# An attention and mixer kernel on one core: token-weight loads behind the first keys, the last product in two halves, a new list of places

## The chip, the cores and the metric

The kernel runs on one core of a Trainium2 chip. The metric is the device time of one execution in microseconds (us); less is better. The times before are from three runs, the profile is one more execution of the same program.

## The reference

Four batches, 12 heads, 448 positions, 64 numbers a head. Causal attention, then a mixer over the positions ("tokens") and one over the 768 channels, both with a residual:

```python
scores = np.where(mask, -1e9, scale * np.matmul(q, k.transpose(0, 1, 3, 2)))
scores = scores - np.max(scores, axis=-1, keepdims=True)
attn = np.exp(scores)
attn = attn / (np.sum(attn, axis=-1, keepdims=True) + 1e-09)
out = np.matmul(attn, v)                       # (B, H, S, D)
x = out.transpose(0, 2, 1, 3).reshape(B, S, H * D)
xt = x.transpose(0, 2, 1)
h = np.maximum(xt @ w_tok1, 0.0) @ w_tok2      # 448 -> 256 -> 448
u = x + h.transpose(0, 2, 1)
h2 = np.maximum(u @ w_ch1, 0.0) @ w_ch2        # 768 -> 1536 -> 768
return u + h2
```

## The kernel before

The heads are worked in 24 pairs, six to a batch. A pair's steps are: load keys, queries and values; turn keys and queries so that the head's 64 numbers lie on the partitions (by VectorE's transpose at L985, or by TensorE at L907 and L913); the scores as small 64x64-tile matmuls (L1018), in two pieces of jobs per pair; for each block of rows "low" (L1040, VectorE: mask and running extreme), the exponential (L1052, ScalarE), a guard and a reciprocal (L1071, L1074) and the scaling; the turn of the probabilities (L1112 on TensorE for the early pairs, through DMA for later ones); the product with the values (L1242, 128x64 tiles, and L1251 for the tips). Of each value load the first rows are copied into a second tile, "vend" (L633 by a helper). Two or more pairs make a slice of x that is turned (L1288) and goes through the token mixer (L1347, relu L1355, L1360, L1380, sum at L1388). The channel mixer works in stages with the up product (L1430 and L1762), and for the last two batches in groups: `group.up` L1833 and `group.down` L1853, whose results are summed into the residual `u` by `add` (L1497). Products are made in three matmuls of 448 columns for a high and a low half of each operand; `narrow` (loads at L685, then L688 on ScalarE, L694 and L698 on VectorE) turns 64-bit weights into such floats.

Channel weights come in loads of 768 KB (`wraw`), keys and queries in four DMAs of 56 KB a tensor (`blocks`, L937; 56 KB as the page counts each), values in three (L946 twice with 96 KB, L950 once), dense rows at L889 and L892. SP issues most DMAs; ScalarE's queue issues some at the start and at the end. The DMAs of these two queues share eight completion semaphores in turn, so that the ninth DMA waits at its queue until the first has landed.

The order of the work is not written out. Every step is a `Job` of a `Plan`; its number in the table `PLACES` is its priority, and a second table, `CHOICE`, gives the engine where several could do it. `Plan.emit` walks a modelled clock, gives each engine the ready job with the lowest number, and so fixes each engine's order of instructions; `keep_warm` (L862) puts filler matmuls into early gaps of TensorE.

At the end of the program the last down products of batches 2 and 3 are handled by `finish` instead of `add`: the sum with the residual in two parts of 224 columns (`plus`, L1875, VectorE), per part the turn by two matmuls on TensorE (L1881), the copy out of PSUM (L631 or L633 by a helper), and a DMA to the output (L1889). The other blocks go by `store`: a transpose on VectorE (L1903) and four DMAs (L1907).

Line numbers here and in the rows are those of the kernel before; in the changed kernel the same lines are one to twelve further down (L685 is L686, L937 is L940, L946 is L949, L1018 is L1021, L1242 is L1245, L1881 is L1893).

Of the kernel before, what the change touches and what calls it, by code (L numbers as in the profile page):

```python
# [21 lines left out]
    "load_pair.blocks": {-2: (1, 2), 10: (124, 153), 12: (201, 252), 14: (234, 266), 16: (288, 343), 18: (405, 422),  # L22
        20: (522, 539), 22: (580, 592), 24: (686, 699), 26: (747, 780), 28: (827, 839), 30: (912, 930), 32: (985,
        1004), 34: (1074, 1080), 36: (1130, 1141), 38: (1204, 1219), 40: (1271, 1331), 42: (1360, 1376), 44: (1404,
        1438)},
    "load_pair.load": {0.5: (8,), 2.5: (9,), 4.5: (174,), 6.5: (219,), 8.5: (306,), 10.5: (332,), 12.5: (392,),
        14.5: (450,), 16.5: (489,), 18.5: (552,), 20.5: (614,), 22.5: (666,), 24.5: (766,), 26.5: (855,), 28.5:
        (899,), 30.5: (971,), 32.5: (1060,), 34.5: (1105,), 36.5: (1192,), 38.5: (1260,), 40.5: (1306,), 42.5:
        (1420,), 44.5: (1489,), 46.5: (1538,)},
    "load_pair.upper": {-0.2: (39,), 1.8: (43,), 3.8: (213,), 5.8: (258,), 7.8: (362,), 9.8: (371,), 11.8: (441,),  # L30
        13.8: (499,), 15.8: (515,), 17.8: (584,), 19.8: (653,), 21.8: (703,), 23.8: (790,), 25.8: (894,), 27.8:
        (928,), 29.8: (1009,), 31.8: (1082,), 33.8: (1131,), 35.8: (1220,), 37.8: (1299,), 39.8: (1329,), 41.8:
        (1449,), 43.8: (1514,), 45.8: (1566,)},
    "narrow.load": {3.5: (0, 3, 19, 52, 60, 102, 106, 150), 12: (282,), 13: (367,), 14: (446,), 15: (508,), 16:
        (606,), 17: (679,), 18: (743,), 19: (819,), 20: (910,), 21: (967,), 22: (1033,), 23: (1100,), 24: (1168,),
        25: (1250,), 26: (1326,), 27: (1400,), 28: (1458,), 29: (1521,), 30: (1564,), 31: (1605,), 32: (1636,), 33:
        (1666,), 34: (1687,), 35: (1723,)},
    "narrow.size": {3.5: (5, 16, 55, 97, 108, 145, 158, 184), 12: (342,), 13: (411,), 14: (490,), 15: (561,), 16:
        (645,), 17: (707,), 18: (775,), 19: (850,), 20: (937,), 21: (1002,), 22: (1071,), 23: (1126,), 24: (1203,),
        25: (1285,), 26: (1364,), 27: (1439,), 28: (1499,), 29: (1550,), 30: (1594,), 31: (1622,), 32: (1653,), 33:  # L40
        (1678,), 34: (1710,), 35: (1743,)},
    "narrow.shift": {3.5: (7, 17, 66, 101, 127, 151, 167, 189), 12: (348,), 13: (427,), 14: (497,), 15: (567,), 16:
        (649,), 17: (712,), 18: (785,), 19: (865,), 20: (946,), 21: (1014,), 22: (1076,), 23: (1133,), 24: (1213,),
        25: (1291,), 26: (1370,), 27: (1446,), 28: (1509,), 29: (1557,), 30: (1599,), 31: (1625,), 32: (1658,), 33:
        (1681,), 34: (1713,), 35: (1751,)},
    "narrow.join": {3.5: (10, 22, 78, 107, 138, 157, 173, 196), 12: (359,), 13: (439,), 14: (501,), 15: (587,), 16:
        (659,), 17: (725,), 18: (788,), 19: (870,), 20: (950,), 21: (1018,), 22: (1077,), 23: (1159,), 24: (1222,),
        25: (1296,), 26: (1372,), 27: (1453,), 28: (1516,), 29: (1558,), 30: (1601,), 31: (1629,), 32: (1664,), 33:
        (1682,), 34: (1716,), 35: (1754,)},
    "token_weights.<lambda>": {3.5: (11, 26, 82, 113, 143, 163, 197, 209)},  # L50
# [482 lines left out]
def kernel(  # L533
# [12 lines left out]
    B, H, S, D = q.shape  # L546
# [1419 lines left out]
```

## Time and profile before

| what | value |
|---|---|
| median of three runs | 543.31 us (542.58 to 543.38) |
| the profiled execution | 543.6 us, of which the span is 541.7 us |
| TensorE clock granted, mean of the profile | 0.999 |
| TensorE busy | 532.4 us (98% of the span), 4377 matmuls |
| VectorE, ScalarE, GpSimd busy | 424.4, 316.2, 164.6 us |
| moved by DMA | 77.72 MB, mean 143 GB/s |

The span runs from the first to the last instruction of the profiled execution, and 1.9 us lie around it. Times in the views are counted from the span's start. PE is TensorE's matmuls, PEld its weight loads, DVE is VectorE, ACT ScalarE, POOL GpSimd, and SPq or ACTq an engine's queue of DMA issues. A row of a timeline gives the start, the duration of the group, and how many instructions it holds; several matmuls run into each other, so that the time one costs is the distance to the next start, not its own duration.

### The profile page before, as it was taken

What the parts mean: (1) busy time and instruction counts of PE and PEld (TensorE: products, weight loads), DVE (VectorE), ACT (ScalarE), POOL (GpSimd) and SP (SyncE); (2) the same over time, 40 slices, a digit from 0 to 9 for tenths busy, and PEclk for the clock granted to TensorE, in tenths of its full rate; (3) what the DMA queues carried; (4) which work ended last, traced back from release to release, by engine and by line L of the source; (5) the groups of instructions that cost most, each with busy time, mean ns of one, the idle gap of its engine ahead of it and who ended that gap; (6) DMA issues with size and microseconds to landing.
All of it is one profiled execution on the core that took longest, in us unless ns stands there. A gap on an engine that the chain in (4) does not pass through costs nothing.

```text
span 541.7 us, 12006 instructions
## 1 busy us (share of the span) xinstructions
PE 532.4 (98%) x4377; PEld 460.3 (85%) x4381; DVE 424.4 (78%) x1032; ACT 316.2 (58%) x765; POOL 164.6 (30%) x221
## 2 busy tenths in 40 slices
PE   7999999999999999999999999999999999999996
PEld 3777887888888888788888999999999999999995
DVE  4997988998998898969878579776787858485664
ACT  4998997999887788978794243343222313141300
POOL 3475744524414413322322353241000310101100
PEclk9999999999999999999999999999999999999999
DMA  8866777999899899889985426648213021212139
GB/s 189 195 119 135 160 221 145 192 198 200 154 233 221 179 186 194 202 186 194 195 242 160 145 88 180 143 120 170 88 30 102 17 87 30 71 50 83 31 55 148
DMA packets 221546, 77.72 MB, mean 143 GB/s; under 512 B 195760, under 2 KB 210992, under 8 KB 221488
## 3 DMA queue, kind: packets, MB, share of 16 engines
q1 hardware_dynamic: 207984, 74.90, 61.3%
q10 hardware_dynamic: 13504, 2.07, 2.4%
q8 instruction: 34, 0.56, 0.4%
q14 instruction: 24, 0.20, 0.1%
HBM read 49.15 MB, written 14.94 MB: 118 GB/s over the span
## 4 chain that ended last, share of the span: by engine, by line
PE 94%; DMA 2%; SPq 2%; ACT 1%; issue 0%; DVE 0%; DVEq 0%
PE ps L1430 33%; PE ps L1853 16%; PE ps L1762 12%; PE ps L1018 7%; PE ps L1242 6%; PE ps L1347 6%; PE ps L1380 6%; PE ps L1833 3%; PE ps L1112 2%; PE ps L1251 2%; PE ps L1288 1%; SPq L937 1%; DMA gl<-in_q_dram 1%; DMA kq<-in_q_dram 1%; DMA wl<-in_moe_w_tok_dram 1%; ACT prob L1052 1%
## 5 line engine op out<-in xcount | busy, mean ns | idle before, releaser
L1497 DVE TENSOR_TENSOR u<-ps,u 128x448 f32<-128x448 f32 x118 | 72.6, 621 | 42.3 <-PE ps L1853 31.0
L1052 ACT ACTIVATE prob<-prob,stat 128x192 f32<-128x192 f32 (+6 forms) x168 | 83.9, 502 | 13.4 <-DVE stat L1040 12.4
L1040 DVE CUSTOM_DVE_ANT_0 prob<-ps,mask 128x320 f32<-128x320 f32 (+6 forms) x168 | 63.6, 414 | 7.3 <-PE ps L1018 6.8
L633 POOL TENSOR_SCALAR prob<-prob,stat 128x64 f32<-128x64 f32 (+6 forms) x86 | 44.3, 527 | 67.2 <-DVE stat L1074 55.4
L631 ACT ACTIVATE wh<-wf 128x768 fp32r<-128x768 f32 x24 | 19.9, 843 | 63.3 <-PE ps L1853 36.3
L1430 PE MATMUL ps<-uh,wh 128*128 128x448 f32 x144 | 54.1, 376 | 0.0
L1430 PE MATMUL ps<-gh,wh 128*128 128x448 f32 x144 | 53.4, 371 | 0.0
L1430 PE MATMUL ps<-gl,wh 128*128 128x448 f32 x144 | 52.7, 366 | 0.0
L1430 PE MATMUL ps<-uh,wl 128*128 128x448 f32 x144 | 52.6, 365 | 0.0
L1430 PE MATMUL ps<-ul,wh 128*128 128x448 f32 x144 | 52.6, 365 | 0.0
L1430 PE MATMUL ps<-gh,wl 128*128 128x448 f32 x144 | 52.4, 364 | 0.0
L1018 PE MATMUL ps<-kq,kq 64*64 64x128 f32 (+5 forms) x768 | 45.9, 358 | 1.1 <-DVE kq L633 0.8
L642 POOL TENSOR_TENSOR wl<-wf,wh 128x768 fp32r<-128x768 f32 x20 | 37.7, 1888 | 26.1 <-ACT wh L631 18.7
L1018 PEld LDWEIGHTS ps<-kq,kq 64*64 64x64 f32 x768 | 26.6, 133 | 18.7 <-issue 10.4
L642 POOL TENSOR_TENSOR pt<-wf,u 128x768 fp32r<-128x768 f32 (+1 forms) x5 | 8.4, 1690 | 104.9 <-ACT u L631 76.9
L1242 PE MATMUL ps<-pt,vraw 128*64 128x128 f32 (+2 forms) x544 | 37.8, 285 | 0.0
L637 ACT COPY pt<-pt 128x512 uint16<-128x512 uint16 (+3 forms) x44 | 36.0, 881 | 0.7 <-DMA pt<-prob 0.6
L1242 PEld LDWEIGHTS ps<-pt,vraw 128*64 128x64 f32 x544 | 28.3, 137 | 9.5 <-issue 2.5
L642 POOL TENSOR_TENSOR ul<-u,uh 128x448 fp32r<-128x448 f32 x19 | 24.4, 1296 | 30.5 <-DVE uh L633 23.0
L1052 ACT ACTIVATION_READ_ACCUMULATOR prob<-prob,stat 128x1 f32 x168 | 32.2, 192 | 0.0
L637 ACT COPY prob<-prob 128x1024 uint16<-128x1024 uint16 (+1 forms) x33 | 30.2, 936 | 1.3 <-POOL prob L633 1.3
L1853 PE MATMUL ps<-u,wh 128*128 128x448 f32 x108 | 30.7, 366 | 0.0
(221 smaller groups left out, 1419.2 us busy)
## 6 DMA issues: line engine op xcount, KB each, us to landing
wraw<-in_moe_w_ch_dram SPq DMA_DIRECT2D x24, 768.0 KB, 5.4
wf<-scratch SPq DMA_DIRECT2D x30, 384.0 KB, 3.3
scratch<-wf SPq DMA_DIRECT2D x24, 384.0 KB, 3.9
vraw<-in_v_dram SPq DMA_DIRECT2D x44, 96.0 KB, 3.6
kq<-in_k_dram SPq DMA_DIRECT2D x60, 56.0 KB, 3.4
kq<-in_q_dram SPq DMA_DIRECT2D x56, 56.0 KB, 2.4
out_dram<-h1h SPq DMA_DIRECT2D x24, 56.0 KB, 1.8
out_dram<-h1l SPq DMA_DIRECT2D x24, 56.0 KB, 2.4
```

The lines of the kernel that those rows point to most:

```text
L633: eng[e].tensor_scalar(dst, src, scale, 0.0, op0=ALU.mult, op1=ALU.add)
L637: nc.scalar.copy(out, in_)
L642: eng[e].tensor_tensor(dst, a, b, op=ALU.subtract)
L1018: nc.tensor.matmul(scores[n].tile[lanes, to:at], lhsT=qe.tile[LANES[j], c * QC:(c + 1) * QC], rhs=ke.tile[LANES[j], slice(*keys)], start=T ...
L1040: nc.vector.tensor_tensor_reduce(out=part(c, r), in0=ps.tile[:, at:at + wide(c)], in1=mask[:, S - QC:S + P] if c == 2 else mask[:, S - wid ...
L1052: nc.scalar.activation(part(c, r), part(c, r), AF.Exp, bias=stat.tile[:, 0, AT[c]:AT[c] + 1], scale=-1.0, accum_out=stat.tile[:, 1, AT[c]: ...
L1242: nc.tensor.matmul(to, lhsT=s.tile[:, kb, j], rhs=rhs, start=(n in first_of), stop=False)
L1347: nc.tensor.matmul(ps.tile[:, :PART], lhsT=w[:, c, m * P:(m + 1) * P], rhs=x.tile[:, c, :], start=(n == 0), stop=(n == len(work) - 1),)
L1430: nc.tensor.matmul(ps.tile[:, :S], lhsT=x.tile[:, at_:at_ + P], rhs=y, start=(n == 0 and i == 0), stop=(n + 1 == w[2] and i == 2),)
L1497: eng[e].tensor_tensor(u, ps.tile[:, :S], u, op=ALU.add)
L1762: nc.tensor.matmul(ps.tile[:, :S], lhsT=l()[:, t * P:(t + 1) * P], rhs=r, start=(t == 0 and n == 0), stop=(t == half - 1 and n == 2),)
L1853: nc.tensor.matmul(ps.tile[:, :S], lhsT=l.tile[:, t * P:(t + 1) * P], rhs=r.tile, start=(n == 0), stop=(n == 3 * len(fs) - 1),)
```

## The change

**Weight loads behind the keys.** `narrow` takes a list of jobs that its load must wait for, and the token weights' loads wait for the job that loads the keys of pair 0:

```diff
-    def narrow(n, shape, source, f, rank, needs=(), raw=None, issues=1):
+    def narrow(n, shape, source, f, rank, needs=(), raw=None, issues=1, behind=()):
...
-        j = plan.job({"sp": 535.0 * issues}, load, holds=[raw], rank=rank, moved=moved, ring=ring, issues=issues)
+        j = plan.job({"sp": 535.0 * issues}, load, needs=behind, holds=[raw], rank=rank, moved=moved, ring=ring, issues=issues)
...
-            a = narrow(w, [P, 1, w], source, f, TRANK, raw=slot(("wh", "wl")[n % 2]), issues=1 + last)
+            a = narrow(
+                w, [P, 1, w], source, f, TRANK, raw=slot(("wh", "wl")[n % 2]), issues=1 + last, behind=raws[0, "k"][1],
+            )
```

**The last down product in two column halves.** For the last group, last column block and last batch the nine matmuls of 448 columns become two jobs of nine matmuls of 224; `finish.plus` of a part needs only its half:

```diff
-        ready = [prev, last] + list(u_split[b, t])
+        ready = (prev if isinstance(prev, list) else [prev] * 2 if final else [prev]) + [last] + list(u_split[b, t])
...
-                def down(e, t=t, b=b, ps=ps):
-                    bank(ps)
+                last = (number, t, b) == (len(GROUPS) - 1, NT - 1, bs[-1])
+                cols = [slice(0, S // 2), slice(S // 2, S)] if last else [slice(0, S)]
+
+                def down(e, t=t, b=b, ps=ps, cols=cols[0]):
+                    if cols.start == 0:
+                        bank(ps)
...
-                                ps.tile[:, :S], lhsT=l.tile[:, t * P:(t + 1) * P], rhs=r.tile,
+                                ps.tile[:, cols], lhsT=l.tile[:, t * P:(t + 1) * P], rhs=r.tile[:, cols],
...
+                prev = []
+                for c in cols:
...
+                    prev.append(plan.job(
+                        {"pe": pe(*[S // len(cols)] * (3 * len(fs)))}, down_,
+                        [z for d in downs for z in d[2:]] + [z for r in gs[b] for z in r[2:]] + prev,
...
-            a = plan.job({"dve": dve1(n * CP)}, plus, ready, [ps, utile[b]], WRANK - 1)
+            a = plan.job({"dve": dve1(n * CP)}, plus, [ready[part]] + ready[2:], [ps, utile[b]], WRANK - 1)
```

**The tables.** `PLACES` and `CHOICE` are replaced as a whole; one entry of the first shows the kind of difference, with the numbers of the values' loads of the first pairs:

```diff
-    "load_pair.load": {0.5: (8,), 2.5: (9,), 4.5: (174,), 6.5: (219,), 8.5: (306,), 10.5: (332,), 12.5: (392,),
+    "load_pair.load": {0.5: (2,), 2.5: (3,), 4.5: (178,), 6.5: (209,), 8.5: (274,), 10.5: (312,), 12.5: (393,),
```

What these do to the order shows at three places. First the start of SP's queue, with the completion semaphores that an issue waits for; `wh` and `wl` are token weights, `uh` and `ul` dense rows of keys and queries for later pairs. Before:

```order
L685 DMA wh_96<-in_moe_w_tok_dram 128x512
L937 DMA kq_99<-in_k_dram 32x14x32 x3
L937 DMA kq_99<-in_k_dram 32x14x32 [waits DMAHW0_49]
L685 DMA wl_113<-in_moe_w_tok_dram 128x512 [waits DMAHW1_49]
L889 DMA uh_115<-in_k_dram 112x8x64 [waits DMAHW2_49]
L889 DMA ul_120<-in_q_dram 112x8x64 [waits DMAHW6_49]
L946 DMA vraw_89<-in_v_dram 128x3x64 [waits DMAHW7_49]
```

and in the change:

```order
L940 DMA kq_96<-in_k_dram 32x14x32 x4
L949 DMA vraw_89<-in_v_dram 128x3x64 [waits DMAHW1_49]
L949 DMA vraw_89<-in_v_dram 128x3x64 [waits DMAHW3_49]
L953 DMA vraw_89<-in_v_dram 64x2x64 [waits DMAHW5_49]
L892 DMA ul_118<-in_q_dram 112x8x64 [waits DMAHW6_49]
L686 DMA wh_124<-in_moe_w_tok_dram 128x512 [waits DMAHW7_49]
L892 DMA uh_128<-in_k_dram 112x8x64 [waits DMAHW0_49]
```

The keys go first and without a wait, the values of pair 0 come up to the second place, and the first token weights to the sixth. On VectorE the two transposes of pair 0 now come first, then the copy of `vend`, then the first low; before, a weight's L694 and L698 came ahead of the transposes and another L694 ahead of the first low.

Second, SP's queue where it loads the keys (`gh`) and queries (`gl`) of pairs 7 and 8 and the first channel weights (`wraw`). Before:

```order
L937 DMA gh_640<-in_k_dram 32x14x32 x4
L946 DMA vraw_91<-in_v_dram 128x3x64 x2
L950 DMA vraw_91<-in_v_dram 64x2x64
L937 DMA gh_738<-in_k_dram 32x14x32 x4
L937 DMA gl_809<-in_q_dram 32x14x32 x4
L937 DMA gl_848<-in_q_dram 32x14x32 x4
L685 DMA wraw_890<-in_moe_w_ch_dram 128x6x256
```

and in the change:

```order
L940 DMA gh_626<-in_k_dram 32x14x32 x4
L949 DMA vraw_91<-in_v_dram 128x3x64 x2
L953 DMA vraw_91<-in_v_dram 64x2x64
L940 DMA gl_728<-in_q_dram 32x14x32 x4
L940 DMA gh_786<-in_k_dram 32x14x32 x4
L940 DMA gl_842<-in_q_dram 32x14x32 x4
L949 DMA vraw_89<-in_v_dram 128x3x64 x2
L953 DMA vraw_89<-in_v_dram 64x2x64
L686 DMA wraw_918<-in_moe_w_ch_dram 128x6x256
```

The query of pair 8 (`gl_848` before, `gl_842` now) stays the last of the four groups, and three value DMAs have come between it and the channel weights. Its last DMA is SP's 59th in the change and was the 60th before.

Third, TensorE at the scores of pair 12. Before, the first piece stands between channel products:

```order
L1430 MATMUL ps_2139<-gh_2097,wl_2109 128x448
L1018 MATMUL ps_2157<-kq_1882,kq_1904 64x448 x2
L1018 MATMUL ps_2158<-kq_1882,kq_1904 64x384 x2
L1018 MATMUL ps_2158<-kq_1882,kq_1904 64x64 x2
L1430 MATMUL ps_2173<-gh_1932,wh_1914 128x448
```

and in the change:

```order
L1245 MATMUL ps_2157<-pt_2065,vraw_89 64x128 x2
L1021 MATMUL ps_2178<-kq_1883,kq_1919 64x448 x2
L1021 MATMUL ps_2179<-kq_1883,kq_1919 64x384 x2
L1021 MATMUL ps_2179<-kq_1883,kq_1919 64x64 x2
L1021 MATMUL ps_2189<-kq_1883,kq_1919 64x320 x2
L1021 MATMUL ps_2190<-kq_1883,kq_1919 64x256 x2
```

Both pieces now stand together (the second begins with `ps_2189`), behind the values' product of an earlier pair and ahead of its tips. Of the 24 pairs 13 have their scores made in one piece like this, where 7 had. Over the whole order the kind of array tile changes 132 times where it changed 156 times; between the second xturn (L1288) and the last product, full tiles give way to 64x64 tiles 5 times (15 before), to 64x128 tiles 4 times (10) and to 128x64 tiles 18 times (13). At the end of TensorE's order come nine half products, the four turns of batch 2, nine half products, and the four turns of batch 3.

## Rows read from the trace of the kernel before

**Rows 1.** The page, busy time and share of each engine.
```profile
PE 532.4 (98%) x4377; PEld 460.3 (85%) x4381; DVE 424.4 (78%) x1032; ACT 316.2 (58%) x765; POOL 164.6 (30%) x221
```

**Rows 2.** Windows: stretch, length, PE, PEld, DVE, ACT, POOL, clock, DMA share, GB/s.
```profile
16.00:24.00 8.00, 7.94 (x139) 5.92 (x138) 8.00 (x33) 8.00 (x31) 4.34 (x10) 1.00 0.78 200
...
100.00:200.00 100.00, 100.00 (x878) 83.42 (x871) 90.27 (x250) 85.53 (x205) 35.23 (x46) 1.00 0.94 195
```

**Rows 3.** Timeline of 0 to 16 us: start, duration, engine, line, tiles, count.
```profile
0.71 2.01 ACTq L937 DMA_DIRECT2D kq<-in_q_dram  x4
...
0.72 0.42 SPq L685 DMA_DIRECT2D wh<-in_moe_w_tok_dram  x1
...
1.20 3.59 SPq L937 DMA_DIRECT2D kq<-in_k_dram  x4
...
4.76 1.15 ACTq L946 DMA_DIRECT2D vraw<-in_v_dram  x2
...
6.40 1.17 DVE L985 STREAM_TRANSPOSE kq<-kq 128x448 f32<-128x448 f32 x2 [0.97 <-DMA kq<-in_k_dram]
...
9.13 0.62 DVE L1040 CUSTOM_DVE_ANT_0 prob<-ps,mask 128x448 f32<-128x448 f32 x1
...
12.64 0.29 DVE L633 TENSOR_SCALAR vend<-vraw 64x256 f32<-64x256 f32 x1
```

**Rows 4.** Line L937 in 0 to 5 us, keys and queries of pair 0.
```profile
DMA to landing us min/median/max: 1.9/3.6/3.8
```

**Rows 5.** Line L946 in 0 to 8 us, the large value loads.
```profile
DMA to landing us min/median/max: 3.1/4.7/5.1
```

**Rows 6.** Waits, 0 to 48 us: total, times, longest.
```profile
DVE kq L985 <- DMA gl<-in_q_dram: 2.1, 1, 2.1
```

**Rows 7.** The chain that ended last, 30 to 56 us: start, us, what.
```profile
42.73 3.77 DMA gl<-in_q_dram
...
46.63 0.13 DVE kq L985
```

**Rows 8.** Line L937 in 33 to 44 us, keys and queries of later pairs.
```profile
DMA to landing us min/median/max: 2.1/2.3/5.6
```

**Rows 9.** The chain over the whole span, pieces between 149 and 192 us.
```profile
149.29 1.22 PE ps L1430 x6
...
169.15 0.92 PE ps L1018 x8
170.07 1.42 PE ps L1430 x6
171.49 0.98 PE ps L1018 x14
...
190.35 1.66 PE ps L1018 x24
```

**Rows 10.** Timeline of PE, 139.3 to 140.2 us.
```profile
139.59 0.36 PE L1430 MATMUL ps<-ul,wh 128*128 128x448 f32 x1
139.80 0.37 PE L1430 MATMUL ps<-uh,wl 128*128 128x448 f32 x1
140.09 0.44 PE L1242 MATMUL ps<-pt,vraw 128*64 128x256 f32 x2
```

**Rows 11.** Timeline of the end, 525 to 542 us.
```profile
534.35 0.57 PE L1853 MATMUL ps<-u,wh 128*128 128x448 f32 x2
...
535.97 0.55 PEld L1881 LDWEIGHTS ps<-ident,u 128*112 128x112 f32 x4
...
536.37 0.69 DVE L1875 TENSOR_TENSOR u<-ps,u 128x224 f32<-128x224 f32 x2 [1.14 <-PE ps L1853]
...
538.00 0.32 ACTq L1889 DMA_DIRECT2D out_dram<-kq  x1
```

**Rows 12.** Line L1889, the four sends at the end.
```profile
DMA to landing us min/median/max: 2.3/2.6/2.8
```

**Rows 13.** The page, a group of instructions: busy, mean ns, idle before and releaser.
```profile
L1040 DVE CUSTOM_DVE_ANT_0 prob<-ps,mask 128x320 f32<-128x320 f32 (+6 forms) x168 | 63.6, 414 | 7.3 <-PE ps L1018 6.8
```

More of the change, by code (lines that the diff above doesn't have):

```diff
@@ L236 @@
[L236 to L241 removed]
+    "load_pair.blocks": {-2: (0, 1), 10: (129, 153), 12: (193, 224), 14: (242, 259), 16: (338, 293), 18: (405, 420),
+        20: (522, 537), 22: (578, 591), 24: (670, 694), 26: (742, 758), 28: (831, 851), 30: (911, 927), 32: (996,
+        1006), 34: (1056, 1070), 36: (1141, 1151), 38: (1205, 1220), 40: (1280, 1293), 42: (1333, 1348), 44: (1406,
+        1426)},
@@ new lines @@
+    "load_rows.load": {0: (7, 4), 2: (10, 23), 4: (30, 45), 6: (68, 79), 8: (105, 91)},
+    "turn_rows.turn": {0.5: (35, 19), 2.5: (64, 76), 4.5: (84, 90), 6.5: (117, 124), 8.5: (169, 148)},
+    "turn_rows.evac": {0.5: (43, 46), 2.5: (81, 88), 4.5: (98, 99), 6.5: (147, 170), 8.5: (188, 190)},
+    "xturn.turn": {1: (208,), 5: (318,), 9: (462,), 13: (593,), 17: (655,), 21: (804,), 25: (947,), 29: (1098,), 33:
+        (1237,), 37: (1382,), 41: (1535,), 45: (1664,)},
+    "xturn.hi": {1: (217, 221), 5: (324, 326), 9: (474, 477), 13: (600, 612), 17: (663, 664), 21: (811, 813), 25:
+        (951, 953), 29: (1102, 1104), 33: (1245, 1249), 37: (1398, 1399), 41: (1544, 1548), 45: (1667, 1668)},
@@ new lines @@
+    "channels.down": {28.5: (697,), 28.75: (703,), 29: (769,), 29.25: (733,), 29.5: (815,), 29.75: (759,), 36:
[6 rows of a table added]
+    "add.plus": {-6: (706, 717, 781, 747, 837, 771, 1079, 1130, 1064, 1093, 1137, 1202, 1143, 1146, 1217, 1271,
[6 rows of a table added]
+    "store.turn": {-5: (1760, 1743, 1775, 1767, 1791, 1792, 1834, 1841, 1852, 1857, 1865, 1874, 2232, 2233, 2238,
+        2244, 2245, 2249, 2254, 2258, 2262, 2266)},
+    "store.send": {-5: (1763, 1746, 1778, 1770, 1793, 1799, 1836, 1845, 1854, 1862, 1868, 1876, 2234, 2237, 2241,
+        2246, 2253, 2250, 2256, 2259, 2265, 2267)},
@@ new lines @@
+    "combined.sum_.do": {-4.94: (1884, 1886, 1889, 1891), -4.93: (1957, 1960, 1964, 1969), -4.92: (2019, 2020, 2022,
+        2024), -4.91: (2087, 2088, 2092, 2096), -4.9: (2143, 2146, 2156, 2162)},
+    "group.product.do": {55.44: (1882,), 55.71: (1887,), 55.98: (1916,), 56.25: (1899,), 56.52: (1920,), 56.79:
[5 rows of a table added]
+    "group.first.do": {-6: (1888, 1949, 2017, 2081, 2158)},
+    "group.plus.do": {-6: (1921, 1923, 1922, 1925, 1931, 1937, 1943, 1991, 1994, 1997, 2005, 2006, 2001, 2009, 2063,
+        2065, 2067, 2072, 2075, 2070, 2078, 2128, 2130, 2131, 2142, 2144, 2134, 2148, 2188, 2189, 2205, 2208, 2209,
+        2206, 2211)},
@@ L242 @@
+    "spared.hi": {-4.9: (2178, 2218)},
+    "spared.lo": {-4.9: (2180, 2222)},
+    "finish.plus": {-6: (2269, 2270, 2272, 2280)},
+    "finish.turn": {-6: (2271, 2273, 2279, 2282)},
+    "finish.evac": {-6: (2275, 2276, 2281, 2284)},
+    "finish.send": {-6: (2277, 2278, 2283, 2285)},
 }
@@ L288 @@
+    "combined.split.lo": {-4.94: "dddd", -4.93: "dddd", -4.92: "dpdd", -4.91: "pdpp", -4.9: "dppd"},
+    "spared.lo": {-4.9: "pd"},
+    "finish.evac": {-6: "ddad"},
 }
```

294 lines of the change are left out of this document (130 added, 164 removed), and 195 rows, old and new, of tables (CHOICE, PLACES).

## The prediction

> **What bounds the kernel now.** I read the busy line of the page first. TensorE works 532.4 of 541.7 us [rows 1], and over 100 to 200 us it works 100.00 of 100 while VectorE is at 90.27 and ScalarE at 85.53 [rows 2]: from about 48 us on the time is the sum of TensorE's steps, and only a shorter step, or a gap filled, is worth anything. Before that it is another kernel: in 16 to 24 us VectorE and ScalarE are both at 8.00 of 8 [rows 2]. So I price three pieces by three views: the start by its timeline and chain, the long middle by the distance between starts of consecutive matmuls, and the end by its timeline. All sums are made against the profiled execution, 543.6 us, which is 0.3 above the median of 543.31.
>
> **The first keys and values.** Today SP issues a token-weight load at 0.72 and the first keys only from 1.20, with a wait in the middle [rows 3]; the keys land just before VectorE's two transposes at 6.40, and the first score minimum (L1040, "low") runs at 9.13 [rows 3], 2.73 later. With the change the four key DMAs are issued first, from 0.72, without a wait, the last near 2.3. Landings took 1.9 to 3.8 [rows 4], so the keys are there at 4.2 to 6.1; I take the middle, 5.2, and the low could follow at 5.2 + 2.73 = 7.9. But in the new order a copy of the values' first rows stands on VectorE between the transposes and the first low. It needs the two large value DMAs of SP, and these wait for the landings of the first and second keys DMA. The first lands near 0.72 + 3.8 = 4.5, and value issues took 1.15 for two on ScalarE's queue [rows 3], so the second goes at about 5.1. Values took 3.1 to 5.1 to land [rows 5]; I take 3.7, nearer the least, because no weight load is in flight with them any more, but three other value DMAs are. The copy takes 0.29 (the second vend copy of [rows 3]). The first low is then at 5.1 + 3.7 + 0.29 = 9.1, as today, with ends of 5.1 + 3.1 + 0.29 = 8.5 (0.6 earlier) and 5.1 + 5.1 + 0.29 = 10.5 (1.4 later). So the wait that names the change wins nothing by itself: the copy behind the values is late next. The token-weight steps that ran before the first low (TensorE needs their result much later) are only put behind it and stay in VectorE's sum.
>
> **The eighth pair's query.** What the start is worth is decided at 46 us. VectorE sat idle 2.1 us for the query of pair 8 [rows 6], and the chain runs through SP's queue: its last DMA goes at 42.73, takes 3.77, and the transposes start at 46.63 [rows 7]. Two things move here. In the new order of SP's DMAs, counted from the top, one DMA fewer stands ahead of that last issue (58 against 59), 0.5 us by the four query issues in 2.01 of [rows 3], so 42.2. And the 768 KB channel-weight load, issued right behind it today, stands three value DMAs later. The loads of this form landed in 2.3 at the median of 33 to 44 us, 5.6 at most [rows 8]; the 3.77 is one that shared the engines with the weights. 42.2 + 2.3 and the 0.13 from landing to transpose give 44.6. VectorE for its part would have been free at 46.63 - 2.1 = 44.5 with today's work ahead, and what stands ahead of it in the new order is the same to within 0.1 us from the first low on, by the durations of before. I take 44.8, 1.8 us earlier. Ends: with the values 0.6 earlier 44.0, a gain of 2.6; with the first low 1.4 later and the landing still 3.77 it is 42.2 + 1.4 + 3.77 + 0.13 = 47.5, a loss of 0.9. **Start: -1.8 (-2.6 to +0.9).**
>
> **The dense middle.** The matmuls are the same; only their neighbours differ. A change of the array's tile (128x128 to 64x64, 128x64 or 64x128 and back) costs a step. In the chain six product matmuls between products take 1.22, but between two pieces of scores 1.42 [rows 9]: 0.20 for out and in. For the other two kinds the nearest row is the step from a product into 128x64, 0.29 from 139.80 to 140.09 where the step before it was 0.21 [rows 10]; the way in alone is 0.08 there, much like half of the 0.20, and I give them the same 0.20 for in and out. Counted in the two orders from the second xturn to the last product, full-array work is left for a tile 38 times before and 27 times in the change: 64x64 goes from 15 to 5, 64x128 from 10 to 4, 128x64 from 13 to 18. 11 x 0.20 = 2.2. Six more pairs, 13 against 7, have their scores made in one piece. A pair in two pieces takes 0.92 + 0.98 = 1.90, one made whole 1.66 [rows 9]; at most 0.24 for each would come on top, 6 x 0.24 = 1.4. Whether those are separate steps or the same ones seen from the other side the rows don't tell, so the ends are 2.2 and 3.6, and I take 2.5: the steps added up along the new order, each with its price in this trace, give 2.3 without the second part. **Middle: -2.5 (-3.6 to -2.2).**
>
> **The end.** The last product's nine matmuls start at 534.35, and the second "plus" of the last batch starts half of 0.69 after 536.37 [rows 11], so 2.37 after the product's start. In the change come nine half matmuls, the four turns of batch 2, nine more halves. A half can't go below half of 0.20, and the four weight loads of the turns take 0.55, about 0.12 apiece when the 0.19 of the last is taken off [rows 11]; I take 0.11 for a half and for a turn. 18 x 0.11 + 4 x 0.11 = 2.42, and from the last step's end to the plus it is 0.22 today (534.35 and nine steps of 0.20 are 536.15, the plus is at 536.37), which makes 2.64: the last plus, and with it the last send at 538.00 [rows 11], is 0.27 later. What is earlier is the stores: on VectorE the first of their transposes stand behind two sums (L1497) of the last group in place of four, so the queues are nearer to empty when the last send starts. That one took 2.8, the longest of the four, the shortest 2.3 [rows 12]. -0.5 + 0.27 is -0.2; ends are +0.3 if it still takes 2.8, and -0.7 with the 1.9 of [rows 4]. **End: -0.2 (-0.7 to +0.3).**
>
> **Sum:** 543.6 - 1.8 - 2.5 - 0.2 = 539.1, and 538.8 on the scale of the median. The fillers change by one matmul at the very start and cost nothing there; the new places and engines shift at most 2 us of work per engine over the whole, which TensorE's full row in [rows 2] hides.
>
> **Rivals.** *The start gives nothing.* The wait only reorders the same bytes: the values take the weights' place, land late, and pair 8's query still arrives at 46.5. For it speaks the long landing of the values [rows 5]; against it that the weight load no longer follows the query. 543.31 - 2.7 = 540.6. *The values do not hold VectorE.* If they land in 2.3, like the loads of [rows 8], the copy is done at 7.7, the low goes at 7.9, 1.2 earlier than I took it, and the gain becomes 5.7: 537.6. Against it stand the 3.1 to 5.1 of [rows 5]. The Trainium skill's page "SBUF — State Buffer", section "The DMA setup-cost knee", would have it so: it gives a transfer about 2 us plus its bytes over 436 GB/s, which is an estimated 2.2 us for 96 KB; the value loads of this trace, at 3.1 or more, do not agree. *Slower: the whole pairs wait.* A pair's scores in one piece need all four probability buffers and score banks of an earlier pair back, where a pair in two pieces needs half at a time. If VectorE is behind, TensorE stops in front of each of the 13. One low is 0.414 on average [rows 13]. The gain of 4.5 is gone at 4.5 / 13 = 0.35 of wait each, and from 5.6 / 13 = 0.43, a little over one low, the kernel is slower; with two lows each it is 10.8, so 549.6. VectorE's 90.27 of 100 speaks for it; against it, TensorE is full there with 7 whole pairs already, and low waits for TensorE (6.8 of its 7.3 us of idle time [rows 13]), not the other way. A wait between 0.26 and 0.43 leaves no measurable difference, around 543.3.
>
> **Chances.** 0.2% of the time, 1.1 us, is about what a measurement can tell from no change. The forecast has 0.56, a start without gain 0.18, values that don't hold 0.08: together faster, 0.82. The half-eaten middle has 0.10 (same), the waiting pairs 0.08 (slower). The range goes from -6.9, all three low ends, 536.4, to the high ends of the sum, +0.9 - 2.2 + 0.3 = -1.0, 542.3; the waiting pairs and most of the no-difference case lie outside.
>
> **What would show it.** In the profile after: the first low at 8.5 to 10.5, with VectorE waiting for a value DMA and not for a weight step; pair 8's transposes at about 44.8, no 2.1 us wait there; the distance from them to the end of the group products shorter by 2.5 with TensorE still full from 48 us; the last plus 2.6 us after the last product starts, the last send landing in 2.3. It is wrong if TensorE's row shows gaps between 48 and 330 us (the waiting pairs), or if the first low comes at 7.9 (no hold by values), or if pair 8's query still ends the wait at 46.5.

## The result and the profile after

| | before | after | ratio, 95% interval |
|---|---|---|---|
| median of the runs | 542.94 us (542.52 to 543.38, 4 runs) | 537.85 us (537.60 to 538.04, 4 runs) | 0.9906 [0.9894, 0.9919] |
| profiled execution | 543.6 us, span 541.7 | 538.04 us, span 536.2 | |

The change makes the kernel 5.1 us faster, by medians. The forecast was 538.8 (536.4 to 542.3), faster. The two spans differ by 5.5 us, and the sections below account for these 5.5. First the busy line of the page after, beside [rows 1]:

```profile
PE 529.8 (99%) x4391; PEld 460.6 (86%) x4391; DVE 426.4 (80%) x1030; ACT 314.0 (59%) x768; POOL 164.2 (31%) x220
```

and its windows (stretch, length, then busy time and count of PE, PEld, DVE, ACT, POOL, granted clock, DMA share, GB/s), beside [rows 2]:

```profile
16.00:24.00 8.00, 7.96 (x142) 6.07 (x139) 7.63 (x32) 8.00 (x31) 4.99 (x10) 1.00 0.84 201
...
48.00:528.00 480.00, 480.00 (x3635) 425.00 (x3636) 384.24 (x868) 274.27 (x637) 139.22 (x159) 1.00 0.65 144
```

and the long stretch in the kernel before:

```profile
48.00:528.00 480.00, 480.00 (x3643) 421.21 (x3640) 380.53 (x871) 277.34 (x636) 139.92 (x163) 1.00 0.62 141
```

TensorE is full over 48 to 528 us, after as before. So the middle became shorter by shorter steps and not by gaps filled, and no whole pair of scores makes TensorE wait. Over the whole span its busy time fell by 2.6 us and its idle time by 2.9.

**The start.** The timeline after, 0 to 9 us (start, duration, engine, line, operation, tiles; in brackets the idle time before and what ended it), beside [rows 3]:

```profile
0.72 1.95 SPq L940 DMA_DIRECT2D kq<-in_k_dram  x4
...
1.49 5.15 PE L865 MATMUL ps<-mask 128*128 128x512 bf16 x16 [1.49 <-POOL mask L650]
...
2.82 1.05 SPq L949 DMA_DIRECT2D vraw<-in_v_dram  x2
...
4.94 1.17 DVE L988 STREAM_TRANSPOSE kq<-kq 128x448 f32<-128x448 f32 x2 [4.94 <-DMA kq<-in_k_dram]
...
6.57 1.79 PE L1021 MATMUL ps<-kq,kq 64*64 64x448 f32 x32
...
6.64 0.29 DVE L634 TENSOR_SCALAR vend<-vraw 64x256 f32<-64x256 f32 x1 [0.53 <-DMA vraw<-in_v_dram]
...
7.70 0.62 DVE L1043 CUSTOM_DVE_ANT_0 prob<-ps,mask 128x448 f32<-128x448 f32 x1 [0.77 <-PE ps L1021]
```

The two large value loads are asked for from 2.82 on, where the forecast had 4.5 and 5.1, and land early; their copy (`vend`) is done at 6.93. The first low, at 7.70, waits for TensorE's scores, and these start when the sixteen fillers ahead of them (L865) are done. How long keys and queries, and then the large value loads, took to land, beside [rows 4, 5]:

```profile
DMA to landing us min/median/max: 2.1/2.5/2.9
```

```profile
DMA to landing us min/median/max: 2.8/3.1/3.3
```

Pair 8, in the chain after, beside [rows 7] (start, us, what):

```profile
39.21 3.46 DMA gh<-in_k_dram
...
44.87 0.53 DVE kq L988
```

The query's transposes start at 44.87, where the forecast had 44.8, and wait for nothing; before it was 46.63. In this one execution VectorE waited for the same pair's keys, which took 3.46 to land:

```profile
DVE kq L988 <- DMA gh<-in_k_dram: 1.2, 1, 1.2
```

In six more profiles with the same start (among the experiments below) VectorE waits for no load there. The query lands 0.2 to 1.8 us before VectorE comes to it, and the transposes stand 35.6 to 36.2 us behind the first low, so that VectorE's own work decides. In the changed kernel profiled again, with its first low at 8.33, no idle time is put before them:

```profile
43.96 0.64 DVE L988 STREAM_TRANSPOSE kq<-gl 128x448 f32<-128x448 f32 x1
```

The second xturn (L1291), from which I count the middle, is at 46.26 against 47.70 before: 1.4 us. From there to the last product it is 482.8 us against 486.65: 3.9. And the end, whose timeline stands below, is 7.20 against 7.39: 0.2. That is 5.5.

### The profile page after: what moved, and what is told of

Read it like the earlier page. It is cut to its first block, busy times and chain, and to the rows that moved or that the text cites. A ratio compares the mean times of both kernels' runs of the same rounds, so it can differ in the third digit from the quotient of the medians.

```text
span 536.2 us, 12037 instructions
## 1 busy us (share of the span) xinstructions
PE 529.8 (99%) x4391; PEld 460.6 (86%) x4391; DVE 426.4 (80%) x1030; ACT 314.0 (59%) x768; POOL 164.2 (31%) x220
## 4 chain that ended last, share of the span: by engine, by line
PE 94%; SPq 2%; DVE 2%; ACT 1%; DMA 1%; issue 0%; POOL 0%; DVEq 0%; POOLq 0%
PE ps L1433 33%; PE ps L1860 16%; PE ps L1765 12%; PE ps L1021 6%; PE ps L1245 6%; PE ps L1383 6%; PE ps L1350 6%; PE ps L1836 3%; PE ps L1254 1%; PE ps L1115 1%; PE ps L1291 1%; SPq L940 1%; PE ps L865 1%; ACT prob L1055 1%; DMA gh<-in_k_dram 1%; PE ps L910 0%
## 5 line engine op out<-in xcount | busy, mean ns | idle before, releaser
L643 POOL TENSOR_TENSOR wl<-wf,wh 128x768 fp32r<-128x768 f32 x26 | 49.5, 1904 | 94.4 <-ACT wh L632 59.4
L1043 DVE CUSTOM_DVE_ANT_0 prob<-ps,mask 128x128 f32<-128x128 f32 (+6 forms) x168 | 63.3, 415 | 7.3 <-PE ps L1021 6.9
L632 ACT ACTIVATE wh<-wf 128x768 fp32r<-128x768 f32 x27 | 22.5, 846 | 51.2 <-PE ps L1860 25.8
L1021 PE MATMUL ps<-kq,kq 64*64 64x64 f32 (+5 forms) x768 | 45.4, 356 | 0.0
L1795 DVE TENSOR_TENSOR kq<-kq,ps 128x448 f32<-128x448 f32 x35 | 21.2, 619 | 14.8 <-PE ps L1765 14.2
L638 ACT COPY pt<-pt 128x384 uint16<-128x384 uint16 (+3 forms) x41 | 31.6, 830 | 0.8 <-DMA pt<-prob 0.8
L1860 PE MATMUL ps<-u,wh 128*128 128x448 f32 (+1 forms) x110 | 31.0, 363 | 0.0
L1433 PEld LDWEIGHTS ps<-uh,wh 128*128 128x128 f32 x144 | 27.0, 188 | 2.8 <-issue 0.2
L1433 PEld LDWEIGHTS ps<-gl,wh 128*128 128x128 f32 x144 | 27.1, 188 | 2.5 <-DVE gl L1468 0.2
```

The lines of the kernel that those rows point to most:

```text
L643: eng[e].tensor_tensor(dst, a, b, op=ALU.subtract)
L1021: nc.tensor.matmul(scores[n].tile[lanes, to:at], lhsT=qe.tile[LANES[j], c * QC:(c + 1) * QC], rhs=ke.tile[LANES[j], slice(*keys)], start=T ...
L1043: nc.vector.tensor_tensor_reduce(out=part(c, r), in0=ps.tile[:, at:at + wide(c)], in1=mask[:, S - QC:S + P] if c == 2 else mask[:, S - wid ...
L1433: nc.tensor.matmul(ps.tile[:, :S], lhsT=x.tile[:, at_:at_ + P], rhs=y, start=(n == 0 and i == 0), stop=(n + 1 == w[2] and i == 2),)
L1860: nc.tensor.matmul(ps.tile[:, cols], lhsT=l.tile[:, t * P:(t + 1) * P], rhs=r.tile[:, cols], start=(n == 0), stop=(n == 3 * len(fs) - 1),)
```

## Experiments

"Measured" gives the median of a run, its lowest and highest time, and the ratio to the kernel before, which was run beside them with medians of 542.78, 542.41 and 542.85. Every other time below is of the profiled execution. `put(a, before=b)` moves the step `a` in the written-out order of all steps to just before the step `b`, `behind=b` to just behind it; nothing else moves. `narrow.load` 3.5 are the first token-weight loads.

### Undoing the first part: weights ahead of the keys

```diff
+    put(("narrow.load", 3.5, 0), before=("load_pair.blocks", -2.0, 0))
+    put(("narrow.load", 3.5, 1), before=("load_pair.load", 0.5, 0))
```

> The changed kernel with one thing undone: the first two token-weight loads go back to their old places on SP's queue, one ahead of the first keys and one right behind them, ahead of the values; every other instruction keeps its order. Theory A (the load ahead of the keys is what held the start): the keys land some 1.4 us later, the first low goes from 7.7 back to between 8.5 and 9.2, and the whole start follows, so that the second xturn stands near 47.7 instead of 46.5 and the time is 1.0 to 1.4 us longer, about 539.1. Theory B (what my prediction said: the wait wins nothing by itself, the start is decided by the queue and by VectorE's order before pair 8): the first low may come later, the second xturn stays within 0.4 us of 46.5 and the time stays within 0.4 of 537.85.

Measured: 538.98 (538.34 to 539.53), ratio 0.9927 [0.9913, 0.9941]. Its timeline:

```profile
6.68 1.17 DVE L988 STREAM_TRANSPOSE kq<-kq 128x448 f32<-128x448 f32 x2 [6.68 <-DMA kq<-in_k_dram]
...
9.29 0.29 DVE L634 TENSOR_SCALAR vend<-vraw 64x256 f32<-64x256 f32 x1 [1.44 <-DMA vraw<-in_v_dram]
...
9.61 0.62 DVE L1043 CUSTOM_DVE_ANT_0 prob<-ps,mask 128x448 f32<-128x448 f32 x1
```

Here the low stands behind the values' copy, as the forecast had it for the change itself. Between the first low and the second xturn it is 37.51 us here (9.61 to 47.12), and 37.48 in the changed kernel profiled again (below; 8.33 to 45.81): what the first low loses arrives whole at 46 us. With the weight loads back, the keys and queries of pair 0 take 2.6 to 3.8 us to land, and 2.1 to 2.9 in the change. Putting the keys first is worth 0.9 to 1.1 us by the medians (against 538.09 and 537.85 for the change). The size is uncertain, because the intervals of the ratios overlap.

### The first part alone, on the kernel before

```diff
+    put(("load_pair.load", 0.5, 0), behind=("load_pair.blocks", -2.0, 0))
+    put(("narrow.load", 3.5, 0), behind=("load_pair.load", 0.5, 0))
+    put(("narrow.load", 3.5, 1), behind=("load_rows.load", 0.0, 0))
+    at = ("heads.expo", 0.0, 0)
+    for n in (0, 1):
+        for name in ("narrow.size", "narrow.shift", "narrow.join", "token_weights.<lambda>", "token_weights.rest_of"):
+            put((name, 3.5, n), behind=at)
+            at = (name, 3.5, n)
```

> The kernel before with the first part of the change alone, order by hand: keys, values of pair 0, then the first two token-weight loads on SP, and the weights' steps on ScalarE, VectorE and GpSimd put behind the first exponential; all else as before. Theory A (keys first is what the start gained): first low near 7.7, second xturn at 46.5, time 1.0 to 1.4 us shorter than before, about 541.7. Theory B (SP's queue up to pair 8's query decides): first low near 7.7, but pair 8's query lands where it did (46.5), second xturn at 47.5 to 47.8, time within 0.3 of before. In both the stretch from the second xturn to the end is as before, 494.0 us.

Measured: 545.59 (544.28 to 547.22), ratio 1.0052 [1.0032, 1.0073], so slower. VectorE in its timeline:

```profile
8.19 0.62 DVE L1040 CUSTOM_DVE_ANT_0 prob<-ps,mask 128x448 f32<-128x448 f32 x1 [2.05 <-PE ps L1018]
...
11.66 0.28 DVE L1040 CUSTOM_DVE_ANT_0 prob<-ps,mask 128x128 f32<-128x128 f32 x1
```

The first low is 0.9 earlier than before, but I had put the weights' steps right behind it, and the second low stands behind them until 11.66 (the first of these steps waits 1.17 for ScalarE). TensorE works only 4.54 us of the next 8, and its granted clock, the third number from the end in the windows, reads 0.94 and then 0.85:

```profile
8.00:16.00 8.00, 4.54 (x76) 3.10 (x68) 5.97 (x23) 5.55 (x19) 3.59 (x7) 0.94 1.15 246
16.00:24.00 8.00, 7.47 (x118) 5.38 (x117) 7.04 (x33) 6.97 (x24) 1.59 (x5) 0.85 0.94 202
```

So this run mixes the part with my own placing of the weights, and I tried it again with each weight's steps spread out:

```diff
-    at = ("heads.expo", 0.0, 0)
-    for n in (0, 1):
+    for n, at in ((0, ("heads.recip", 0.0, 0)), (1, ("heads.low", 2.0, 0))):
```

> The kernel before with the keys and values first on SP, as in the second experiment, but with the steps of the first two token weights placed where the changed kernel has them, behind the first reciprocal and the second pair's first low. Theory A (keys first alone brings the first part of the start's gain): first low at 7.7 to 8.4 instead of 9.1, the second xturn 38.6 behind it as before, so at 46.3 to 47.0, time 0.7 to 1.2 shorter than before. Theory B (without the refitted places the gain is given back): second xturn at 47.5 or later, time no shorter than before.

Measured: 544.73 (543.87 to 546.47), ratio 1.0036 [1.0019, 1.0053]. The granted clock stays at 1.00 in the profiled execution, which was the shortest of the twelve; over the three longest it reads 0.991 to 0.992 on average, so part of this median is the clock. The first low comes at 8.81, but VectorE has no time left for the steps that were put off:

```profile
16.00:24.00 8.00, 7.38 (x122) 5.30 (x124) 8.00 (x38) 7.71 (x26) 3.57 (x9) 1.00 0.90 214
...
32.00:40.00 8.00, 8.00 (x177) 6.21 (x175) 8.00 (x29) 7.93 (x29) 6.73 (x15) 1.00 0.56 103
```

VectorE is at 8.00 of 8 from 16 to 40 us (24 to 32 too), and the second xturn comes at 48.22 where it was 47.70. In these two placings the keys alone gain nothing. I take the gain to come with the fitted order, which puts the weights' steps into VectorE's holes (7.63 of 8 in 16 to 24 us above), but no run tests that by itself. That no placing in the old order would gain isn't shown.

### Four of the sixteen fillers left out

After the runs above the first low looked to be set by the fillers, so I removed the last four ahead of the first scores; their results are read by nobody.

```diff
+    first = [n for n, (j, _) in enumerate(todo) if j.tag == ("heads.<lambda>", 0.0, 0)][0]
+    fill = [n for n in range(first) if todo[n][0].tag is None]
+    for n in fill[12:][::-1]:
+        todo.pop(n)
```

> The changed kernel without the last 4 of the 16 filler matmuls that stand ahead of the first scores on TensorE; all else in the same order. Seen so far in seven executions: the fillers take 0.43 us each until the clock rises and 0.215 after, the rise comes anywhere between 4.6 and 7.5 us, the first scores start between 6.57 and 7.99, and in six of the seven the second xturn stands 37.5 us behind the first low. Theory A (the fillers are what the first scores wait for): first scores at 6.1 to 6.7 in every execution, first low at 7.2 to 7.8, second xturn at 44.7 to 45.3, time 0.4 to 1.0 shorter than the changed kernel, about 537.2, and the executions closer together. Theory B (fewer fillers leave the clock low for longer): the first scores take 3 us instead of 1.8, the first low comes no earlier, and the time is the same or longer.

Measured: 538.09 (537.08 to 538.94), ratio 0.9906 [0.9881, 0.9932], no measurable difference from the change. Its timeline:

```profile
7.26 0.62 DVE L1043 CUSTOM_DVE_ANT_0 prob<-ps,mask 128x448 f32<-128x448 f32 x1 [0.37 <-PE ps L1021]
...
8.49 0.99 PE L916 MATMUL ps<-ident,ul 112*64 112x112 f32 x16 [0.58 <-DMA ul<-in_q_dram]
```

The scores start at 6.12 and the low comes at 7.26, the earliest of all, but TensorE is then done at 7.91 and stands until 8.49 before the dense rows (`ul`), which haven't landed. The second xturn is at 45.70, 38.44 behind the low and not 37.5. So four fillers fewer gain nothing: the dense rows are late next.

### Channel weights right behind pair 8's query again

```diff
+    put(("narrow.load", 12.0, 0), before=("load_pair.load", 8.5, 0))
```

> The changed kernel with one DMA moved: the first channel-weight load goes right behind pair 8's query on SP's queue, as it stood before, ahead of the three value DMAs. Theory A (my prediction: that load stretches the query's last landing from 2.3 to 3.8): the transposes of pair 8's query wait for it, the distance from the first low to the second xturn grows from 37.5 to about 38.6, time 0.5 to 1.1 longer. Theory B (VectorE's order decides, the query is there before VectorE comes to it): distance 37.5 to 37.8, time within 0.3 of the changed kernel.

Measured: 539.94 (537.72 to 542.65), ratio 0.9951 [0.9930, 0.9972]: about 2 longer than the change, and spread wider. Not by the way I expected: the query isn't late (the second xturn is at 46.13, 37.53 behind the first low). The load that now follows the weights is, in its chain and its waits:

```profile
43.78 4.38 DMA vraw<-in_v_dram
```

```profile
POOL vend L634 <- DMA vraw<-in_v_dram: 2.7, 1, 2.7
...
PE ps L1115 <- POOL prob L634: 1.2, 1, 1.2
```

The values of pair 8 take 4.38 to land, GpSimd waits 2.7 for them with the probabilities' scaling queued behind, VectorE waits 2.2 for GpSimd, and TensorE 1.2. The three value loads take 4.2 to 4.5 each in this execution, and 2.2 to 3.9 in the profiles where the 768 KB load stands behind them, so it does hold what is queued behind it here. Beside the changed kernel profiled again, TensorE loses 1.7 between 50 and 53 us and 0.6 at a later wait near 153 us, which together are about the 2 us of the medians. That its old place had cost the query 3.77 [rows 7] is not shown by this.

### Ten whole pairs split again

In ten of the pairs whose scores are made in one piece, one product was moved between the two pieces, which brings nine of the changes from full array to tile back.

```diff
+    second = lambda g: ("heads.<lambda>", 2.0 * g, 1)
+    for g, tag in (
+        (8, ("channels.up", 27.0, 0)), (10, ("channels.up", 27.667, 0)), (12, ("channels.down", 29.25, 0)),
...
+    ):
+        put(tag, before=second(g))
```

> The changed kernel with ten whole pairs taken apart again: for each, one product that stands behind (for pair 8 to 23) is moved between its two pieces of scores; nothing is added or left out, and full-array work gives way to a tile 9 times more often. Theory A (a way into a tile and back costs three steps: about 0.09 on the way in, 0.11 for the first full matmul after, and 0.11 to 0.15 for the last tile matmul before it): 9 x 0.35 = 3.2 us longer than the changed kernel beside it. Theory B (my prediction: 0.20 for in and out, nothing else): 9 x 0.20 = 1.8 us longer.

Beside it ran the changed kernel again, unedited:

> The changed kernel again, every instruction in the same order, as the yardstick for the three kernels beside it and for how much the start moves from one execution to the next. All theories: 537.9 within 0.5, the last product's start 482.3 to 482.8 us after the second xturn, second xturn between 45.4 and 46.7.

Measured: 543.42 (542.47 to 544.49), ratio 1.0012 [0.9999, 1.0025]: the whole gain is gone, 5.3 more than the change run again (538.09, 537.15 to 538.22, ratio 0.9909 [0.9892, 0.9926]). This kernel has 3 whole pairs left, fewer than the 7 before, and gives way to a tile 36 times (38 before). Both theories were too small. Pair 8 in the chain of the change run again (first) and of the split kernel; each has 32 score matmuls, of which the chain counts some:

```profile
80.24 1.56 PE ps L1021 x26
81.80 1.41 PE ps L1383 x6
83.21 1.21 PE ps L1433 x6
84.42 1.21 PE ps L1383 x6
85.64 0.58 PE ps L1115 x14
```

```profile
81.07 0.76 PE ps L1021 x9
81.82 1.43 PE ps L1433 x6
83.25 0.98 PE ps L1021 x14
84.23 2.63 PE ps L1383 x12
86.86 0.58 PE ps L1115 x14
```

The same work takes 5.40 in one piece and 5.79 split: the product 1.43 and not 1.21 (0.22 for in and out, as in [rows 9]), and the scores 0.76 + 0.98 = 1.74 and not 1.56 (0.18 more). **The two are separate steps and add up.** From the second xturn to the last product it is 487.95 against 482.24, 5.7 more; three gaps of TensorE, together 1.06, take part of it, and the rest is 0.47 for each of the ten pairs.

### A visit to a tile by itself

To price the change of tile without moving anything, 72 small matmuls were added ahead of channel products, once as 64x64 tiles and once, at the same places, over the whole array. In the traces 65 of them stand between two full products (50 behind a channel product, 15 behind one of the token mixer) and 7 behind a tile matmul, where the expectations take 50 and 22.

```diff
+            if n == 0:
+                nc.tensor.matmul(ps.tile[:64, S:S + 64], lhsT=still[:64, :64], rhs=still[:64, :64], start=True, stop=True)
```

```diff
+            if n == 0:
+                nc.tensor.matmul(ps.tile[:, S:S + 64], lhsT=still[:, :P], rhs=still[:, :64], start=True, stop=True)
```

> The changed kernel with 72 matmuls added, each on a 64x64 tile with 64 columns in unused columns of the bank that the product behind it fills; their result is read by nobody. 50 stand between two full-array matmuls, 22 between a tile and a full matmul. Theory A: 50 x (0.35 + nothing, since the last tile step is the matmul itself) + 22 x 0.04 = 18.4 us longer than the changed kernel. Theory B: 50 x (0.20 + 0.04) + 22 x 0.04 = 12.9 us longer.

> The control for the added tile matmuls: 72 matmuls at the same places, also 64 columns, but on the full 128x128 array, their result read by nobody. Both theories: no change of tile at the 50 places between full matmuls, each costs its own step, 0.10 to 0.12 as the shortest full-array steps in the trace do, so 7 to 9 us longer than the changed kernel; the 22 behind a tile the same, as they take over the way out. What the tile matmuls cost above their own step is then the price of a visit.

Measured: 560.35 (559.90 to 560.82), ratio 1.0323 [1.0303, 1.0342], and 544.71 (544.24 to 546.76), ratio 1.0038 [1.0021, 1.0055]. Against the change run again that is 22.3 longer, more than either theory, and 6.6, a little less than expected. One visit of each in the timeline:

```profile
155.72 0.37 PE L1435 MATMUL ps<-uh,wl 128*128 128x448 f32 x1
156.02 0.21 PE L1432 MATMUL ps<-mask 64*64 64x64 bf16 x1
156.16 0.47 PE L1435 MATMUL ps<-uh,wh 128*128 128x448 f32 x1
156.47 0.37 PE L1435 MATMUL ps<-ul,wh 128*128 128x448 f32 x1
```

```profile
154.03 0.37 PE L1435 MATMUL ps<-uh,wl 128*128 128x448 f32 x1
154.24 0.20 PE L1432 MATMUL ps<-mask 128*128 128x64 bf16 x1
154.28 0.45 PE L1435 MATMUL ps<-uh,wh 128*128 128x448 f32 x1
154.57 0.37 PE L1435 MATMUL ps<-ul,wh 128*128 128x448 f32 x1
```

Read the distances between starts: 0.30 into the tile, 0.14 for it, 0.31 for the first full product behind it, in all 0.75, where the two products alone take 0.41. So a visit of a single tile matmul costs 0.34. Over the full array the three are 0.21, 0.04 and 0.29: 0.13. With 65 such places this comes out at the medians: 65 x 0.34 = 22.1 of 22.3, and 65 x 0.13 = 8.5 against 6.6. The difference, 0.21 by the timelines and 0.24 by the medians, is near the 0.20 that the forecast took for out and in; the other 0.13 is what a matmul as small as this costs there in either form. The Trainium skill's page "TensorEngine Tiling (Array Packing)", section "Key Properties", says that a change of the tiling mode drains TensorE, without a price. These runs agree that a change costs time, and give a price; whether a drain is the reason they don't show.

### The end: halves undone, and halves without turns between them

The last product whole again, with the places and engines of the steps behind it to match:

```diff
-    "finish.plus": {-6: (2269, 2270, 2272, 2280)},
+    "finish.plus": {-6: (2269, 2270, 2272, 2273)},
...
-    "finish.evac": {-6: "ddad"},
+    "finish.evac": {-6: "adad"},
...
-                cols = [slice(0, S // 2), slice(S // 2, S)] if last else [slice(0, S)]
+                cols = [slice(0, S)]
```

> The changed kernel with the last product made whole again and the end ordered as before (product, turns of batch 2, turns of batch 3; the four copies alternate between ScalarE and VectorE); nothing ahead of it differs. Theory A (my prediction's split: the halves cost, the earlier stores pay): the last send starts 3.65 us after the last product's start, as before, instead of 4.3, and still lands in about 2.0, so the end is 0.4 to 0.7 shorter, time about 537.3. Theory B (the halves are what shortens the end): the end is 0.3 or more longer, time 538.2 or more.

Measured: 537.79 (537.21 to 538.64), ratio 0.9907 [0.9891, 0.9924]. And the halves kept, but the four turns of batch 2 moved behind the second:

```diff
-    "finish.turn": {-6: (2271, 2273, 2279, 2282)},
+    "finish.turn": {-6: (2274.2, 2274.4, 2279, 2282)},
```

> The changed kernel with one thing moved: the four turns of batch 2 stand behind both halves of the last product instead of between them. Theory A (the turns between the halves push the last sum, as priced at 0.44 and measured at 0.65): the last sum comes 2.2 us after the last product's start instead of 2.94, and the end is 0.4 to 0.7 shorter, time about 537.3. Theory B (the chain is then held by VectorE's copies of batch 2, or by the sends queued together): the gain is under 0.2.

Measured: 537.22 (536.86 to 538.50), ratio 0.9901 [0.9885, 0.9917]. All of them against the last product's first matmul, which is at 529.05 after (other distances worked out in the same way from each timeline):

| | last plus | last send starts | last send landed | end |
|---|---|---|---|---|
| before | 2.33 | 3.65 | 6.48 | 7.39 |
| after | 2.94 | 4.31 | 6.29 | 7.20 |
| last product whole | 2.33 | 3.68 | 6.31 | 7.22 |
| turns behind the halves | 2.51 | 4.00 | 6.42 | 7.32 |

The timeline of the end after, beside [rows 11], and the landing of its four sends, beside [rows 12]:

```profile
529.05 0.38 PE L1860 MATMUL ps<-u,wh 128*128 128x224 f32 x2
...
530.04 0.60 PE L1893 MATMUL ps<-ident,u 128*112 128x128 f32 x4
...
530.69 0.48 PE L1860 MATMUL ps<-u,wh 128*128 128x224 f32 x2
...
531.99 0.39 DVE L1887 TENSOR_TENSOR u<-ps,u 128x224 f32<-128x224 f32 x1 [0.69 <-PE ps L1860]
```

```profile
DMA to landing us min/median/max: 1.9/2.0/2.0
```

Its chain runs from the first half through VectorE's sum of that half to the second half:

```profile
530.24 0.40 DVE u L1887
...
530.69 1.28 PE ps L1860 x9
```

The turns start 0.11 apart and are done at 530.48. The second half then waits for that sum and starts 0.2 later.

Halving puts the last send 0.66 later and makes it land in 1.98, 0.7 behind the send before it, where two sends that start 0.03 apart in the whole product take 2.46 and 2.66. The two cancel to 0.02. What remains of the end's gain, 0.17, is there without halves: I take it to come from the stores, which are issued earlier (the last at 1.16 from the product's start, before at 1.90), but no run moves them alone. With the turns behind the halves the last plus is 0.43 earlier and the last send 0.31, yet the end is 0.12 later: the last sends took 2.4 each, and five of the stores ahead of them 3.4 to 3.8, where these took 1.9 to 2.2 in the change. Its median of 537.22 is not to be told from the change's.

## Why the prediction was right, and where it was not

**Start: forecast 1.8, measured 1.4 in the profiled execution and 1.1 to 2.3 in six more that have the same start (the second xturn at 45.4 to 46.6). The sum held; its first step did not.** "The first low is then at 5.1 + 3.7 + 0.29 = 9.1, as today" was wrong twice. The value load was taken to wait for a landing of 3.8 as in [rows 4]; with no weight load beside them the keys landed in 2.1 to 2.9 (in 2.6 to 3.8 with the weights ahead again), and SP was free for the values at 2.82. And the values took 2.8 to 3.3, not 3.7. So "the values do not hold VectorE" was right of that wait, and its first low of 7.9 is close to the 7.70 here, by luck: the copy was done at 6.93, and the low waited for the scores. The Trainium skill's page "SBUF — State Buffer", section "The DMA setup-cost knee", from which an estimated 2.2 us followed for 96 KB, is nearer to these landings than to those before, but still below all of them.

But that rival's 537.6, nearer to the measured 537.85 than the forecast is, rested on the low being early for good, and it isn't: TensorE is late next. The scores stand behind sixteen fillers, and a filler takes 0.43 us up to some moment and 0.215 from then on. That moment differs between executions, so the scores started at 6.53 to 7.99 in seven profiles with the same start, and the first low came at 7.66 to 9.12. The forecast had counted the fillers as free.

In the profiled execution nothing was lost by that error, since VectorE waited there for pair 8's keys, and the query came out near the forecast (its last DMA at 42.58, forecast 42.2; the transposes at 44.87, forecast 44.8). That is in part luck. In the six other profiles the query is early, and VectorE's work behind the first low decides: 35.6 to 36.2 us, which the forecast had at 35.4 (44.5 less 9.1). So a low at 9.12, the forecast's 9.1, puts the transposes at 44.78, and one at 7.95 puts them at 43.59. Below that an early low runs into the dense rows, as the run with four fillers less shows. Of the 1.76 gained at the transposes 1.44 is left at the xturn, which stands 1.39 behind them and stood 1.07 behind them before.

How much the start is worth is the least certain of the three. Only one execution of the kernel before was profiled, and it is 0.7 above the median. The medians gain 5.1, and 4.3 where the change was run again; with 3.9 to 4.4 for the middle and 0.2 for the end, that would leave the start between nothing and 1.0. Undoing its first part still costs 0.9 to 1.1.

"The wait that names the change wins nothing by itself" is right in one order and wrong in the other: in the old order the keys first gained nothing in two placings, in the new one taking them back costs 0.9 to 1.1.

**Middle: forecast 2.5, measured 3.9, and 4.3 to 4.4 in five more profiles. This is the term that was mis-sized.** In the profiled execution two steps of scores near 57.5 us took 0.5 longer than in the others. The middle of the order before is steady, 486.60 to 486.74 in three profiles. Its steps, as sums of distances between starts of TensorE's matmuls from the second xturn to the last product, in the kernel before and in the change profiled again:

```
                                        before        change
full products at their own pace         398.93        398.93
above that, the last one before a tile    3.50 (38)     2.45 (27)
above that, the first one after a tile    4.09 (39)     2.93 (28)
other full products                      -0.04          0.23
tile matmuls                             80.17         77.69
sum                                     486.65        482.24
```

The second and third rows fall by 2.2, the 11 x 0.20 of the forecast, and the other full products take 0.3 of it back. The tile matmuls fall by 2.5, and for these the forecast held 0 to 1.4 and took next to nothing: "whether those are separate steps or the same ones seen from the other side the rows don't tell". They are separate, as the split pairs show (0.22 and 0.18 for one pair). Its far end of 3.6 was passed too, since it counted the scores alone, and these give 1.5 of the 2.5; the tips (L1254) give 0.7 and the turns of the probabilities (L1115) 0.2 more, which I take for the same effect but did not test by itself.

**End: forecast 0.2, measured 0.2, by two errors that cancel.** The last plus came 0.6 later, not 0.27. The half steps and the turns, 0.11 each, were right; what the forecast left out is the wait of the second half for VectorE's sum of the first. From 530.04 to 530.69 it is 0.65 where four turns make 0.44, and the second half's first step then takes 0.21 in place of 0.10. The last send landed 0.85 faster, not 0.5.

**Rivals.** The waiting pairs are excluded: no gap of TensorE from 48 to 528 us, and low's idle time before it unchanged, beside [rows 13]:

```profile
L1043 DVE CUSTOM_DVE_ANT_0 prob<-ps,mask 128x128 f32<-128x128 f32 (+6 forms) x168 | 63.3, 415 | 7.3 <-PE ps L1021 6.9
```

The start without gain is excluded for the profiled execution by the transposes at 44.87; how much the start gives by the medians is open, as said above. Measured against the median, the sum was 1 us too high: in the two profiles the middle is short by 1.4 and the start long by 0.4.

## What to carry to other kernels

Where TensorE is full, count tile changes and price them from both sides: the full product beside the tile, and the tile's own steps, which the row of the full product doesn't show; a split pair of scores cost 0.40 to 0.47 us here where one side alone gave 0.20. When the first load is moved forward, ask what is late next on each engine in turn (values, then fillers, then dense rows), and take the price at the point where the stage is decided, not at its first instruction. And before cutting the last product to send a part earlier, ask whether the sends would only land at the same time: here a whole product with the stores out of the way ended as early, and the second half stood waiting for the first half's sum.

## What had not been expected of the hardware

- A filler, 512 columns, takes 0.43 us at first and 0.215 from a later moment on, which are the two levels of TensorE's clock, 1.2 and 2.4 GHz. That moment differs between executions: the same sixteen took 5.15 us in the profile after, 5.77 in the change profiled again, and 6.57 with the whole last product. The granted clock does not show it. Windows after, and with the whole last product:

```profile
4.00:6.00 2.00, 2.00 (x9) 0.88 (x8) 1.06 (x2) 0.69 (x1) 0.00 (x0) 1.00 1.13 236
```

```profile
4.00:6.00 2.00, 2.00 (x6) 0.76 (x5) 1.17 (x2) 0.94 (x1) 0.00 (x0) 1.00 1.14 239
```

  Both read 1.00, and TensorE is full in both, with nine matmuls begun in the one and six in the other. The first low stands at 7.70 in the one and at 9.12 in the other.
- In one run (the first part alone, first placing) the granted clock read 0.94 in 8 us of which TensorE worked 4.54, and 0.85 in the next 8 us, though it was busy again for 7.47 of them; it reads 1.00 in 24 to 32 us.
- One 64x64 matmul of 64 columns between two full products costs 0.34 us, more than the 0.20 step of a full product of 448 columns.
